# A fused attention, MLP and mixture-of-experts kernel: four weight conversions, a register load, transposes and low-part subtractions take other places in the expert phase

## The chip, the cores and the metric

The kernel runs on one core of a Trainium2 chip. Its engines are TensorE (PE in the profile: matmuls and transposes; its weight loads are PEld), VectorE (DVE), ScalarE (ACT), GpSimd (POOL) and SyncE (SP, which issues most transfers). Each engine works through its own instructions in program order; they meet by semaphores. The metric is device time in microseconds (us), the median of several executions.

## The reference

Three stages, each on 2304 tokens of 512 numbers:

```
# 1. attention, 4 x 8 heads, 576 positions of 64, a mask of blocks of 64
scores = np.where(mask, q @ kT * scale, -1e9); attn = softmax(scores); x = attn @ v
# 2. MLP, 512 -> 2048 -> 512
h = x @ w_in;  x = (max(h, 0) + alpha * min(h, 0)) @ w_out
# 3. mixture of 8 experts, 512 -> 1024 -> 512, one expert per token
logits = x @ w_gate;  expert_idx = argmax(logits);  gate_w = softmax(logits)[expert_idx]
for e in range(8):
    mask = expert_idx == e
    out[mask] = gate_w[mask, None] * (max(x[mask] @ w1[e], 0) @ w2[e])
```

## The kernel before

**Precision.** Most matmuls split each float32 operand into a high part (a rounded copy in the type fp32r) and a low part (the rest), and add three products: high by high, high by low, low by high (`pass3`). A weight block of 128 x 512 arrives by DMA in a tile `raw`; ScalarE casts it to the high part, then a subtraction on VectorE or GpSimd makes the low part. That pair is a conversion (`conv`). The tiles of the results are called `e`; an expert has 16 blocks, 0 to 7 for its first layer and 8 to 15 for its second.

**Up to the experts.** Attention and MLP are put in order by a planner (`Plan`), a list scheduler with a fixed cost per task. Its last tasks belong to the last of nine groups of 256 tokens. `first_expert` adds to the same plan the first expert's weights: 16 loads through four `raw` tiles in turn (`NR`), each followed by its conversion.

**The experts.** Behind the plan the program is written out in order by `Experts.run`. Experts come in the order of their token counts, the largest first (r = 0, 1, ...). An expert's tokens are worked in tiles of 256 (`tile256`, called by `body`), and what remains in a tile of 128 or 64. A tile gathers its tokens' rows from DRAM by an indirect DMA into `xg` (`fetch`; the list of rows `it` comes first, by a DMA on SP), turns them with TensorE transposes `Tx` (`xprep`), runs layer 1 (eight steps f, each twelve matmuls into `l`), then hidden values `hh` and `hl`, then layer 2 (two halves h of eight steps into `Y`, 0.70 us each at full clock), and scatters the scaled result to `out`. Between these steps `body` slips in two lists: `jobs`, the conversions of the next expert's weights, one per step; and `ahead`, of which one entry is taken behind every second step of layer 2: the eight places are f = 1, 3, 5, 7 of the first half, then of the second. Tiles that carry jobs have a + in their names.

**The first tile** (0, 0) is special. The last group's routing is done inside it, by hooks `at[n]`: transposes `rt` of the last group's outputs, copies of them back to `xg` (one half by ScalarE, one by VectorE), the gate's logits `lg` behind layer-1 step 1, the ranking matmul `rk` in step 3, two scatters of the token list `info`, then `fetch` of tile (0, 1), `order_all` (the order and the counts of the experts, on VectorE, into `odri`), `known` (SP reads the next expert's number, and the 16 loads of its weights are issued), and `counts` (every engine reads the eight counts into registers, and a branch hint for the branch `few0` that ends the tile).

**What sets the order.** Within an engine only the program order. SP's queue holds the lists `it` and the weight loads; POOL's the gathers and scatters, and its share of the low parts: `conv` sends blocks 2, 5, 8, 11, 14 of the later experts to GpSimd, the others to VectorE. Different paths for different counts are If blocks, each engine branching for itself. In this data the path is: expert 0 in five tiles of 256 (the third with jobs) and one of 128; expert 1 in two (the first with jobs) and one of 64; expert 2 in one with jobs and one of 64; expert 3 in a tile of 128 with jobs; expert 4 in one of 64.

Of the kernel before, what the change touches and what calls it, by code (L numbers as in the profile page):

```python
# [8 lines left out]
F32 = mybir.dt.float32  # L9
# [10 lines left out]
P = 128  # L20
# [11 lines left out]
NRECIP = 4  # L32
NR = 4
RATE = 300
LAG = 2
SC = 1.0 / float(D) ** 0.5
KC = 512 + P
# [254 lines left out]
class Attention:  # L292
# [24 lines left out]
    def plan(A, pl):  # L317
# [4 lines left out]
        for p, c in A.units():  # L322
            left.append(A.unit(pl, p, c, A.prio(p, c), A.soon(p, c), left))
            if (p < HP or A.soon(p, c)) and len(left) > LAG - 1:
                left.pop(0)()
# [21 lines left out]
    def early(A, pl):  # L347
# [3 lines left out]
        for p in range(2 * HP):  # L351
# [11 lines left out]

            got = pl.add(("SP", 450), load, [i], [x], pr + 10 * (p % HP), (P * 2 * EARLY * 4, RATE), [got] if b and p % 2 else ())
            pl.add(("ACT", 400), scale, [i], [x], pr + 5000 - 300 if b == 0 else pr + 600)
            if w not in pl.bufs:
# [5 lines left out]

                pl.add(("SP", 450), loadv, [], [w], pr + 10 * (p % HP) + 5, (131072 * n, RATE))

    def pair(A, pl, p):
# [14 lines left out]

        pl.add(("SP", 450), load, [], [("qk", p)], pr - 600 if p >= HP else 600 * p + 50, (P * QK * 4, RATE))
        pl.add(("SP", 450), loadv, [], [("v", p)], pr - 600 if p >= HP else 600 * p + 50, (327680, RATE))
        if plain:
# [21 lines left out]
    def unit(A, pl, p, c, pr, soon, left):  # L415
# [44 lines left out]
        fn, keys = scores1 if p < NPLAIN or soon else scores, Ss + [("step", 0)]  # L460
        if len(left) == LAG:
            left.pop(0)(ns, fn, ks, keys, pr)
# [466 lines left out]
class Experts:  # L929
# [53 lines left out]
    def conv(A, r, i):  # L983
        hi, lo = A.Ws[r % 2][i]
        raw = A.raw[r, i]
        A.nc.scalar.copy(hi, raw)  # L986
        (A.nc.gpsimd if i % (3 if r > 0 else 6) == 2 else A.nc.vector).tensor_sub(lo, raw, hi.bitcast(F32))  # L987

    def fetch(A, r, j, base, rows=NT + 1):
        it = A.itile(r, j)  # L990
# [164 lines left out]
    def run(A, base, last, order, order_all):  # L1155

        nc = A.nc

        def reg(row, r, top):
            return nc.sync.value_load(order.ri[0:1, row, r:r + 1], min_val=0, max_val=top)

        def xpreps(r, j):
            return [lambda: A.xprep(r, j, 0), lambda: A.xprep(r, j, 1)]

        def hint(label, cond):

            A.tc.mark_branch_hint_location(label, hint=cond, engines=ENGINES)

        def nexts(r, j, b, nb):
            fs = xpreps(r, j) if b is not None else []
            if nb is not None:
                fs += [lambda: A.fetch(r + 1, 0, nb)] + [lambda: None] * (4 - len(fs)) + xpreps(r + 1, 0)
            return fs

        def load_next(r):
            if r < E - 2:
                A.load_raws(r + 2, reg(0, r + 2, E - 1))

        def big(r, j, b, jobs=(), nb=None):
            more = A.TOP[r] > 2 * P * (j + 1)

            if A.TOP[r] > 2 * P * (j + 1) + P and (r, j) != (0, 1):
                hint(f"rest{r}_{j + 1}", ns[r] > 2 * P * (j + 1) + P)
            if more:
                A.fetch(r, j + 1, b)
            A.body(r, j, 2 * P, jobs, nexts(r, j + 1, b if more else None, nb))
            if jobs:
                load_next(r)  # L1190

        def bigs(r, j, b):
            if A.TOP[r] > 2 * P * j + P:
                with A.tc.If(ns[r] > 2 * P * j + P, label=f"rest{r}_{j}"):
                    big(r, j, b)
                    bigs(r, j + 1, b)

        def sized(n, left, go):

            def little():  # L1200
                with A.tc.If(left(0)):
                    go(64)

            if n > 64:
                with A.tc.If(left(64)) as c:
                    go(P)
                with c.Else():
                    little()
            else:
                little()  # L1210

        def remainder(r):

            n = (ns[r] + (P - 1)) & (2 * P - 1)

            def go(size):
                if r + 1 < E:
                    hint(f"less{r + 1}", ns[r + 1] <= P)
                A.body(r, 1, size, it=A.rem)

            sized(P if A.TOP[r] > 2 * P + 64 else 64, lambda k: n > P - 1 + k, go)

        def only(r, nb):

            jobs = [lambda: A.fetch(r + 1, 0, nb)] + [lambda i=i: A.conv(r + 1, i) for i in range(16)] if r < E - 1 else []
            if r < E - 2:
                jobs[-1] = lambda: (A.conv(r + 1, 15), load_next(r))

            def go(size):
                hint(f"more{r}", ns[r] > P)  # L1230
                A.body(r, 0, size, jobs, xpreps(r + 1, 0) if jobs else (), cond=ns[r + 1] > 0 if jobs else None)

            with A.tc.If(ns[r] <= 64) as c:  # L1233
                go(64)
            with c.Else():
                go(P)

        hold = {}

        def known():  # L1240
            hold["e1"], hold["nb"] = reg(0, 1, E - 1), reg(2, 1, (E - 1) * NT)
            A.load_raws(1, hold["e1"])
            A.wtiles(1)

        def counts():
            _, hold["n"] = nc.values_load_multi_w_load_instructions(order.ri[0:1, 1, :], min_val=0, max_val=NT)
            hint("few0", hold["n"][0] <= 5 * P)

        at = dict(last)
        for f in (lambda: A.fetch(0, 1, base), order_all, known, counts):  # L1250
            at[max(at) + 1] = f
        A.body(0, 0, 2 * P, [], [lambda: None] * 5 + xpreps(0, 1), at)
        nb = hold["nb"]
        ns = hold["n"]
        n0 = ns[0]

        def convs(r):
            return [lambda i=i: A.conv(r, i) for i in range(16)]

        with A.tc.If(n0 <= 5 * P, label="few0"):  # L1260
            with A.tc.If(n0 > 3 * P) as c:
                big(0, 1, base, convs(1), nb)
            with c.Else():
                for f in [lambda: A.fetch(1, 0, nb)] + convs(1) + xpreps(1, 0) + [lambda: load_next(0)]:
                    f()
            hint("many0", n0 > 5 * P)
        with A.tc.If(n0 > 5 * P, label="many0"):
            big(0, 1, base)
            big(0, 2, base, convs(1), nb)
            bigs(0, 3, base)  # L1270
        remainder(0)
        with ExitStack() as st:
            for r in range(1, E):
                base = nb
                st.enter_context(A.tc.If(ns[r] > 0))
                nb = reg(2, r + 1, (E - 1) * NT) if r < E - 1 else None
                jobs = convs(r + 1) if r < E - 1 else []
                with A.tc.If(ns[r] <= P, label=f"less{r}"):
                    only(r, nb)
                if r < E - 1:  # L1280
                    st.enter_context(A.tc.If(ns[r] + P * ns[r + 1] > P))
                with A.tc.If(ns[r] > P, label=f"more{r}"):
                    big(r, 0, base, jobs, nb)
                    bigs(r, 1, base)
                    remainder(r)


def moe_kernel(tc, qk, v, qke, ve, w_in, w_out, alpha, w_gate, w1, w2, out):
    nc = tc.nc
    with ExitStack() as ctx:  # L1290
# [15 lines left out]
        pl, banks, hold = Plan(), Slots(), {}  # L1306
# [7 lines left out]
        at = Attention(tc, qk, v, qke, ve, xT)  # L1314
# [38 lines left out]
        def first_expert(done):  # L1353
# [8 lines left out]
            def wload(i):  # L1362
                def f(on):
                    hold["ex"].wload(0, hold["e"], i, hold["ex"].raws[i % NR])
                pl.add(("SP", 450), f, [("e",)], [("raw0", i % NR)], 0, (262144, 180))

            def conv(i):
                pool = i % 6 == 2

                def hi(on):  # L1370
                    ex = hold["ex"]
                    ex.wtiles(0, i, i + 1)
                    nc.scalar.copy(ex.Ws[0][i][0], ex.raw[0, i])

                def lo(on):
                    ex = hold["ex"]
                    h, l = ex.Ws[0][i]
                    (nc.gpsimd if pool else nc.vector).tensor_sub(l, ex.raw[0, i], h.bitcast(F32))

                g, r = NG - 1, ("raw0", i % NR)  # L1380
                free = [("l1", g, 3 + 4 * (i // 8))] if i % 8 < 4 else [("l2", g, i // 8 * 4 + i % 4)]
                pl.add(("ACT", 600), hi, [r, *free], [("eh", i)] + ([("eh", i - 1)] if i else []), 1)
                pl.add(("POOL", 1600) if pool else ("DVE", 580), lo, [r, ("eh", i)], [("el", i)], 1)
# [6 lines left out]
            for i in range(NR):  # L1390
                wload(i)
            for i in range(16):
                conv(i)
                if i + NR < 16:
                    wload(i + NR)
            for i in range(GT):
# [19 lines left out]
        done = list(pl.tasks)  # L1416
        ml.plan(pl)
        first_expert(done)
        pl.emit()
        ex = hold["ex"]  # L1420
# [59 lines left out]
```

## Time and profile before

| | |
|---|---|
| time, median of 3 (lowest to highest) | 960.91 us (960.36 to 966.23) |
| the profiled execution | 963.68 us, span 961.9 us |
| PE busy | 898.5 us (93%) |
| DVE, ACT, POOL busy | 499.6 (52%), 410.0 (43%), 323.2 (34%) |
| mean granted TensorE clock | 0.971 of full speed |

The span runs from the first instruction to the last of the profiled execution; some 2 us of its time lie outside. The expert phase begins at about 652 us. A granted clock of 1.00 is TensorE's level of 2.4 GHz, 0.50 that of 1.2 GHz. Times of instructions overlap by a little, since a matmul's end is modelled.

### The profile page before, as it was taken

How to read it: one execution, taken by the hardware profiler on the slowest of the kernel's cores; microseconds unless marked ns; L12 is line 12 of the kernel's file. 1: busy time of each engine (PE TensorE's matmuls, PEld its weight loads, DVE VectorE, ACT ScalarE, POOL GpSimd, SP SyncE). 2: the span in 40 equal slices, each digit the busy share in tenths (PEclk: the TensorE clock that was granted, in tenths of full speed). 3: DMA queues.
4: the chain of work that ended last, by engine and by line, in shares of the span. 5: the costliest groups of instructions: out<-in, count | busy, mean ns of one | idle time of the engine just before them, and what ended most of it. 6: DMA issues, size and time to landing. Idle time of an engine off the chain costs nothing. (4 is left out here: it accounts for less than half of the span.)

```text
span 961.9 us, 17930 instructions
## 1 busy us (share of the span) xinstructions
PE 898.5 (93%) x6329; PEld 768.1 (80%) x6329; DVE 499.6 (52%) x1194; ACT 410.0 (43%) x1037; POOL 323.2 (34%) x333
## 2 busy tenths in 40 slices
PE   7998989999999999999999999998799998999874
PEld 6656658889888888888999999897698987888764
DVE  4999886656656556655444343455115211514360
ACT  6877765455455445545212121233125222524351
POOL 1455663323343433343223232331214212412340
PEclk9999989999999999999999999997899999999987
DMA  9981002212302122001001010151616211613451
GB/s 343 352 311 52 27 19 75 74 47 70 75 27 75 53 70 77 27 28 53 13 5 41 5 41 1 33 153 57 221 34 202 84 46 56 209 47 108 139 172 49
DMA packets 46268, 85.81 MB, mean 89 GB/s; under 512 B 12191, under 2 KB 18991, under 8 KB 46128
## 3 DMA queue, kind: packets, MB, share of 16 engines
q1 hardware_dynamic: 35264, 64.20, 20.9%
q0 software_dynamic: 4240, 11.56, 3.8%
q10 hardware_dynamic: 6624, 8.39, 2.4%
q8 instruction: 63, 1.03, 0.5%
q14 instruction: 77, 0.63, 0.2%
HBM read 70.85 MB, written 13.67 MB: 88 GB/s over the span
## 5 line engine op out<-in xcount | busy, mean ns | idle before, releaser
L692 PE MATMUL l<-xh,wi 128*128 128x256 f32 x1024 | 205.1, 286 | 0.0
L692 PEld LDWEIGHTS l<-xh,wi 128*128 128x128 f32 x1024 | 166.4, 190 | 4.2 <-issue 0.5
L720 PE MATMUL acc<-wo,gh 128*128 128x512 f32 x512 | 166.7, 407 | 0.0
L692 PE MATMUL l<-xl,wi 128*128 128x256 f32 x512 | 144.6, 282 | 0.1
L698 POOL TENSOR_TENSOR gl<-t,gh 128x256 fp32r<-128x256 f32 x103 | 78.4, 763 | 191.6 <-ACT gh L695 156.7
L670 DVE TENSOR_SCALAR t<-l,al 128x256 f32<-128x256 f32 x128 | 61.9, 484 | 139.3 <-PE l L692 136.1
L695 ACT CAST gh<-t 128x256 fp32r<-128x256 f32 x124 | 50.4, 406 | 184.3 <-DVE t L671 103.7
L528 POOL TENSOR_SCALAR P<-P,sm 128x256 f32<-128x256 f32 (+4 forms) x66 | 78.1, 1190 | 107.2 <-ACT gh L695 41.1
L720 PE MATMUL acc<-wo,gl 128*128 128x512 f32 x256 | 100.8, 394 | 2.7 <-POOL gl L698 2.7
L692 PEld LDWEIGHTS l<-xl,wi 128*128 128x128 f32 x512 | 97.5, 190 | 4.0 <-issue 0.5
L720 PEld LDWEIGHTS acc<-wo,gh 128*128 128x128 f32 x512 | 86.5, 190 | 11.2 <-issue 0.5
L477 DVE TENSOR_REDUCE nb<-S 128x1 f32<-128x256 f32 (+4 forms) x160 | 70.1, 477 | 41.0 <-PE S L454 25.9
L522 ACT COPY F<-PT 128x384 f32<-128x384 f32 (+2 forms) x124 | 57.3, 478 | 54.2 <-PE PT L517 52.8
L494 ACT ACTIVATE P<-S,nb 128x128 f32<-128x128 f32 (+3 forms) x128 | 66.9, 530 | 14.7 <-DVE nb L477 13.5
L517 PE MATMUL PT<-ident,P 128*128 128x128 f32 (+1 forms) x400 | 64.5, 281 | 7.8 <-DVE xo L571 5.4
L1030 PE MATMUL l<-cxh,e 128*128 128x256 f32 x320 | 62.9, 295 | 6.3 <-PEq L1260 4.3
L517 PEld LDWEIGHTS PT<-ident,P 128*128 128x128 f32 (+1 forms) x400 | 46.0, 141 | 21.1 <-DVE xo L571 5.0
L720 PEld LDWEIGHTS acc<-wo,gl 128*128 128x128 f32 x256 | 48.1, 188 | 14.9 <-POOL gl L698 4.0
L1030 PEld LDWEIGHTS l<-cxh,e 128*128 128x128 f32 x320 | 53.4, 202 | 7.1 <-issue 6.9
L671 DVE SCALAR_TENSOR_TENSOR t<-l,t 128x256 f32<-128x256 f32 x128 | 54.3, 425 | 4.4
L1030 PE MATMUL Y<-e,hh 128*128 128x512 f32 x176 | 56.3, 401 | 0.0
L987 DVE TENSOR_TENSOR e<-raw,e 128x512 fp32r<-128x512 f32 x44 | 40.2, 933 | 26.4 <-ACT e L986 26.3
(374 smaller groups left out, 1721.1 us busy)
## 6 DMA issues: line engine op xcount, KB each, us to landing
raw<-in_moe_w_dram SPq DMA_DIRECT2D x96, 256.0 KB, 3.7
qk<-in_qk_dram SPq DMA_DIRECT2D x16, 608.0 KB, 4.8
rawi<-in_moe_w_in_dram SPq DMA_DIRECT2D x16, 512.0 KB, 10.3
rawo<-in_moe_w_out_dram SPq DMA_DIRECT2D x16, 512.0 KB, 8.4
v<-in_v_dram SPq DMA_DIRECT2D x16, 320.0 KB, 3.2
x<-y ACTq DMA_DIRECT2D x16, 256.0 KB, 2.0
xr<-xT SPq DMA_DIRECT2D x7, 512.0 KB, 3.8
qe<-in_qke_dram SPq DMA_DIRECT2D x8, 256.0 KB, 4.4
```

The costliest lines, as they stand in the source:

```text
L477: nc.vector.tensor_reduce(pl["nb", p, c][:, 2 * k + j:2 * k + j + 1], pl[Ss[j]][:, a:b], axis=AX.X, op=ALU.max, negate=True)
L494: nc.scalar.activation(pl[x][:, a:b], pl[Ss[j]][:, a:b], AF.Exp, bias=nb, scale=1.0, accum_out=pl["sm", p, c][:, 2 * k + j:2 * k + j + 1])
L517: nc.tensor.transpose(pl[t][0:w, k], pl[x][:, P * k:P * k + w], A.K.ident)
L522: f(pl[F][:, 0:n], pl[t][:, 0:n])
L528: (nc.gpsimd if on == "POOL" else nc.vector).tensor_scalar(y, y, pl["sm", p, c][:, k:k + 1], None, op0=ALU.mult)
L670: nc.vector.tensor_scalar(pl[out], x, 0.0, A.K.al[:, f:f + 1], op0=ALU.min, op1=ALU.mult)
L671: nc.vector.scalar_tensor_tensor(pl[out], x, 0.0, pl[out], op0=ALU.max, op1=ALU.add)
L692: nc.tensor.matmul(pl[l][:, 0:G], lhsT=a[:, c], rhs=b, start=k == 0 and j == 0, stop=k == 3 and j == 2)
L695: (nc.scalar.copy if on == "ACT" else nc.vector.tensor_copy)(pl[gh], pl[t])
L698: (nc.gpsimd if on == "POOL" else nc.vector).tensor_sub(pl[gl], pl[t], pl[gh].bitcast(F32))
L720: nc.tensor.matmul(pl[acc], lhsT=x[:, c], rhs=w, start=f == 0 and j == 0, stop=f == 15 and j == 2)
L1030: A.nc.tensor.matmul(ps, lhsT=x[a], rhs=w[b], start=first and q == 0, stop=last and q == 2)
```

## The change

Four edits. The first expert's last four blocks (12 to 15, `FIRST`) are no longer converted in the plan but by hooks of the first tile (`late`), behind `known`. `counts` moves from a hook in layer 1 to the third place of `ahead`, and the loads of expert 1's weights move from `known` to the fourth, so behind `counts`. In later tiles the lists of `ahead` begin with an empty place (`nexts`), which puts every turn one place later, and the fetch for the next expert with it. All low parts go to VectorE.

```diff
         raw = A.raw[r, i]
         A.nc.scalar.copy(hi, raw)
-        (A.nc.gpsimd if i % (3 if r > 0 else 6) == 2 else A.nc.vector).tensor_sub(lo, raw, hi.bitcast(F32))
+        A.nc.vector.tensor_sub(lo, raw, hi.bitcast(F32))
...
         def nexts(r, j, b, nb):
-            fs = xpreps(r, j) if b is not None else []
+            fs = [lambda: None] + xpreps(r, j) if b is not None else []
             if nb is not None:
-                fs += [lambda: A.fetch(r + 1, 0, nb)] + [lambda: None] * (4 - len(fs)) + xpreps(r + 1, 0)
+                fs += [lambda: A.fetch(r + 1, 0, nb)]
+                fs += [lambda: None] * (6 - len(fs)) + xpreps(r + 1, 0)
...
             hold["e1"], hold["nb"] = reg(0, 1, E - 1), reg(2, 1, (E - 1) * NT)
-            A.load_raws(1, hold["e1"])
             A.wtiles(1)
...
+        def late(i):
+            A.wtiles(0, i, i + 1)
+            A.conv(0, i)
+
-        for f in (lambda: A.fetch(0, 1, base), order_all, known, counts):
+        for f in [lambda: A.fetch(0, 1, base), order_all, known] + [lambda i=i: late(i) for i in range(FIRST, 16)]:
             at[max(at) + 1] = f
-        A.body(0, 0, 2 * P, [], [lambda: None] * 5 + xpreps(0, 1), at)
+        ahead = [lambda: None] * 2 + [counts, lambda: A.load_raws(1, hold["e1"]), lambda: None] + xpreps(0, 1)
+        A.body(0, 0, 2 * P, [], ahead, at)
...
             for i in range(16):
-                conv(i)
+                if i < FIRST:
+                    conv(i)
                 if i + NR < 16:
```

The instructions of the plan keep their order on every engine; only the four conversions are taken out of it.

ScalarE in the first tile, before. `e_12` to `e_15` are the casts of the last four blocks, `xg<-rt` the copy that the logits need.

```order
L1373 CAST e_11_7959<-raw_6034 128x512
L1399 DMA x_58<-yo_6018 128x512
L1373 CAST e_12_7964<-raw_6031 128x512
L1373 CAST e_13_7967<-raw_6032 128x512
L1373 CAST e_14_7970<-raw_6033 128x512
L1373 CAST e_15_7973<-raw_6034 128x512
L861 COPY xg<-rt_0_8006 128x512
L814 ACTIVATE ex_8046<-L_8035 128x16
L1052 ACTIVATE hh_6023<-l_0_256_0_7993 128x512
```

The four casts stood ahead of the copy. The same stretch of ScalarE after the change:

```order
L1379 CAST e_11_7959<-raw_6034 128x512
L1406 DMA x_58<-yo_6018 128x512
L862 COPY xg<-rt_0_7994 128x512
L815 ACTIVATE ex_8034<-L_8023 128x16
L1053 ACTIVATE hh_6023<-l_0_256_0_7981 128x512
L1053 ACTIVATE hh_6025<-l_0_256_1_8046 128x512
L987 CAST e_12_8181<-raw_6031 128x512
L1053 ACTIVATE hh_6027<-l_0_256_2_8097 128x512
L987 CAST e_13_8193<-raw_6032 128x512
L987 CAST e_14_8202<-raw_6033 128x512
L987 CAST e_15_8211<-raw_6034 128x512
L1053 ACTIVATE hh_6029<-l_0_256_3_8186 128x512
```

The copy now follows the cast of block 11, and the four casts stand around the third and fourth `hh`; their subtractions stand in the same places on VectorE, behind `order_all`.

SP before, from the last of the 16 loads for expert 1 to the branch `few0` (`odri` is the tile of the counts):

```order
L976 DMA raw_7991<-in_moe_w_dram 128x512
L1246 TENSOR_LOAD odri
L1246 ISA x16
L1169 REGISTER_ALU
L1475 BRANCH_PREFETCH_HINT
L1260 COMPARE_AND_BRANCH
L1261 COMPARE_AND_BRANCH
```

SP read the counts behind its loads. After the change, from the reads of `known` to the first of the 16 loads:

```order
L1163 ISA x2
L1247 TENSOR_LOAD odri
L1247 ISA x16
L1170 REGISTER_ALU
L1482 BRANCH_PREFETCH_HINT
L977 ISA
L977 DMA raw_6031<-in_moe_w_dram 128x512
```

SP reads them first, and the loads start behind that. POOL reads them behind the gathers of tile (0, 1) in both.

VectorE in the tile of 128 of expert 3 (a + tile), up to the first `hl`, before. The branches stand around the jobs.

```order
L987 TENSOR_TENSOR e_0_7695<-raw_6031,e_0_7695 128x512
L987 TENSOR_TENSOR e_1_7727<-raw_6032,e_1_7727 128x512
L987 TENSOR_TENSOR e_3_7785<-raw_6034,e_3_7785 128x512
L1019 UNCONDITIONAL_BRANCH x2
L1019 COMPARE_AND_BRANCH
L987 TENSOR_TENSOR e_4_7811<-raw_7980,e_4_7811 128x512
L987 TENSOR_TENSOR e_6_7851<-raw_7982,e_6_7851 128x512
L1019 UNCONDITIONAL_BRANCH x2
L1082 TENSOR_TENSOR hl_6024<-Th_0_128+_0_14668,hh_6023 128x512
```

After the change:

```order
L988 TENSOR_TENSOR e_1_7727<-raw_6032,e_1_7727 128x512
L988 TENSOR_TENSOR e_2_7757<-raw_6033,e_2_7757 128x512
L988 TENSOR_TENSOR e_3_7785<-raw_6034,e_3_7785 128x512
L1020 UNCONDITIONAL_BRANCH x2
L1020 COMPARE_AND_BRANCH
L988 TENSOR_TENSOR e_4_7811<-raw_7968,e_4_7811 128x512
L988 TENSOR_TENSOR e_5_7832<-raw_7969,e_5_7832 128x512
L988 TENSOR_TENSOR e_6_7851<-raw_7970,e_6_7851 128x512
L1020 UNCONDITIONAL_BRANCH x2
L1083 TENSOR_TENSOR hl_6024<-Th_0_128+_0_14668,hh_6023 128x512
```

Seven subtractions now stand ahead of `hl` instead of five (block 0 is the row above the piece); blocks 2 and 5 have left GpSimd.

## Rows read from the trace of the kernel before

**Rows 1.** TensorE's timeline, 640 to 962 us: start, us, instruction [idle before, releaser]

```profile
658.56 3.59 PE L793 MATMUL lg<-wg,xg 128*128 128x8 f32 x16 [2.75 <-ACT xg L861]
...
673.14 0.36 PE L1030 MATMUL l<-cxh,e 128*128 128x256 f32 x1 [2.03 <-issue]
...
676.04 0.62 PE L1030 MATMUL Y<-e,hh 128*128 128x512 f32 x2
...
685.02 0.63 PE L1003 MATMUL Tx<-ident,xg 128*128 128x128 f32 x4 [0.42 <-DMA xg<-x,it]
...
688.09 0.63 PE L1003 MATMUL Tx<-ident,xg 128*128 128x128 f32 x4 [1.04 <-DMA xg<-x,it]
...
694.43 0.55 PE L1030 MATMUL l<-cxh,e 128*128 128x256 f32 x1 [4.31 <-PEq L1260]
...
733.96 0.63 PE L1003 MATMUL Tx<-ident,xg 128*128 128x128 f32 x4 [1.21 <-DMA xg<-x,it]
...
794.03 0.70 PE L1030 MATMUL H<-e,cxh 128*128 128x512 f32 x2 [1.17 <-ACTq L1194]
...
898.28 0.63 PE L1003 MATMUL Tx<-ident,xg 128*128 128x128 f32 x4 [0.88 <-DVE e L987]
...
925.32 0.80 PE L1030 MATMUL Y_128+_14687<-e,hl 128*128 128x512 f32 x1 [3.47 <-DVE hl L1082]
...
936.78 1.23 PE L1113 MATMUL H_64+_0_15724<-e,cxh 128*128 128x256 f32 x8 [2.10 <-DVEq L1282]
```

**Rows 2.** ScalarE's timeline, 655 to 659 us

```profile
657.40 0.62 ACT L1373 CAST e<-raw 128x512 fp32r<-128x512 f32 x1 [0.88 <-DMA raw<-in_moe_w_dram]
657.92 0.58 ACT L861 COPY xg<-rt 128x512 f32<-128x512 f32 x1
```

**Rows 3.** Windows: length, busy PE, PEld, DVE, ACT, POOL, granted clock, DMA share, GB/s

```profile
655.80:668.00 12.20, 9.45 (x45) 9.45 (x45) 4.31 (x19) 2.42 (x5) 1.48 (x2) 0.59 0.07 26
...
694.40:699.00 4.60, 4.57 (x22) 4.60 (x23) 0.00 (x0) 0.00 (x0) 0.00 (x0) 0.52 0.37 141
720.00:746.00 26.00, 24.80 (x163) 21.78 (x162) 13.62 (x20) 14.17 (x26) 11.82 (x11) 1.00 0.59 192
...
925.30:930.70 5.40, 5.38 (x19) 4.71 (x20) 2.20 (x4) 1.87 (x4) 0.00 (x0) 0.50 0.78 250
```

**Rows 4.** GpSimd's timeline, 668 to 682 us and 916 to 925 us

```profile
669.50 1.05 POOL L853 DMA_INDIRECT info<-ig,si  x1 [11.34 <-DVE ig L850]
673.22 0.98 POOL L853 DMA_INDIRECT info<-ig,si  x1 [2.67 <-DMA info<-ig,si]
679.94 0.98 POOL L996 DMA_INDIRECT xg<-x,it  x1 [5.74 <-DMA it<-info]
681.23 0.97 POOL L996 DMA_INDIRECT xg<-x,it  x1 [0.30 <-issue]
...
920.38 3.73 POOL L987 TENSOR_TENSOR e<-raw,e 128x512 fp32r<-128x512 f32 x3
```

**Rows 5.** SP's issues, 668 to 682 us

```profile
676.65 0.39 SPq L992 DMA_DIRECT2D it<-info  x1
...
679.38 2.67 SPq L976 DMA_DIRECT2D raw<-in_moe_w_dram  x5
```

**Rows 6.** VectorE's timeline, 668 to 682 us and 908 to 940 us

```profile
671.58 0.17 DVE L925 CAST odri<-odres 1x24 int32<-1x24 f32 x1
...
916.93 1.30 DVE L987 TENSOR_TENSOR e<-raw,e 128x512 fp32r<-128x512 f32 x2 [1.07 <-ACT e L986]
...
920.61 4.06 DVE L987 TENSOR_TENSOR e<-raw,e 128x512 fp32r<-128x512 f32 x1 [0.35 <-ACT e L986]
...
931.30 5.28 DVE L987 TENSOR_TENSOR e<-raw,e 128x512 fp32r<-128x512 f32 x5
```

**Rows 7.** DMA issues, 754 to 764 us: count, median us to landing

```profile
xg<-x,it POOLq DMA_INDIRECT x2, 3.3
```

**Rows 8.** DMA queues, 691 to 692 us: packets, MB, share of 16 engines

```profile
q8 instruction: 1, 0.02, 5.9%
```

## The prediction before the run

> **What bounds the kernel now.** TensorE is busy for 93% of the span, and up to 652 us the change leaves every instruction in its place, so I read only the expert phase, and there TensorE's idle time first: its timeline, for the rows that carry a bracket. [rows 1] holds those that the change can touch: 2.75 us ahead of the logits, 2.03 and 0.42 and 1.04 later in the first tile, 4.31 at the branch that ends it, 1.21 and 0.88 ahead of transposes, 3.47 and 2.10 around the tile of 128 of expert 3. The windows come second, for the granted clock: behind three of these waits TensorE ran at about its lower level, 0.59, 0.52 and 0.50 of full speed [rows 3], so such a wait costs more than its length. Third come the timelines of the engines named in the brackets, to see what stood in their queues.
>
> **The sum is made against the profiled execution**, 963.68 us with a span of 961.9; it lies 2.77 above the median of 960.91. I take the same number of microseconds off the median.
>
> **The first tile: logits.** ScalarE's copy of `xg` ran at 657.92, right behind the cast of the last block at 657.40, which itself waited for its transfer [rows 2]. TensorE had come to the logits at 655.81 (658.56 less 2.75). With the four casts out of the way the copy follows the transposes, which TensorE had finished well ahead of its step 1; the wait goes: 2.75 us. With it goes, I take it, the lower clock: between 655.80 and 668.00 TensorE was busy for 9.45 us, from the logits on all of it at half speed, which is 4.7 us at full. Some 4.05 of these 4.7 lie ahead of the end of `rk`, at 666.7 (8.1 us after 658.56, halved). So the end of `rk` moves by 2.75 + 4.05 = 6.8, to 659.9.
>
> **What is late next: the chain of the token list.** From `rk` two scatters of the list on POOL (669.50, 673.22) [rows 4], then the DMA of `it` on SP at 676.65 [rows 5], then the gathers at 679.94 and 681.23 follow each other, each waiting for the transfer before. None of these gaps holds work that the change takes out, so the chain keeps its length: gathers at 673.1 and 674.4. Their landing: before, the transposes could start 5.1 and 6.9 us after the issue (685.02, 688.09), with the weight loads in flight from 679.38; in a quiet stretch a gather lands in 3.3 us [rows 7]. The loads now wait for SP's read of the counts. SP's price for that shows in no row here; the nearest is TensorE's, which had `odri` at 671.75 [rows 6] and went on at 673.14, 1.39 later. Loads then start at 679.38 - 6.8 + 1.4 = 674.0, 0.9 behind the first gather instead of 0.6 ahead of it. For the first gather I take 3.9 us (between 3.3 and 5.1, nearer to quiet): 677.0. For the second, which meets the loads, 5.1 (between 3.3 and 6.9): 679.5.
>
> TensorE's own way from the end of `rk` to the first transpose was 684.60 - 666.7 = 17.9 us, with 2.03 of waiting at `counts` and 0.65 of low clock in it; without both it stands there at 675.1, and with a read of the counts of at most 1.39, which no longer waits for `odri`, at 676.5 at the latest. So the gathers bind: it waits 0.5 to 1.9 us for the first, then about 0.5 for the second (677.0 + 2.03 of work against 679.5), and ends at 679.5 + 2.03 = 681.5. Before it ended at 690.12 (694.43 less 4.31). **The first tile: 8.6 us less**; with both gathers as slow as before 6.8, with both in time and a free read 10.9 (675.1 + 4.06 = 679.2).
>
> **The four late conversions** cost nothing while their cover holds. VectorE ends `odri` 5.06 us after `rk`, at 665.0; then come four subtractions of 0.65 [rows 6] with two `hl` of the same size among them, 3.9 us in all: done at 668.9. Layer 2 starts at 676.04 - 666.7 - 2.03 - 0.65 = 6.7 after `rk`, at 666.6, and needs blocks 14 and 15 from its seventh step, at 666.6 + 6 x 0.70 = 670.8. The slack is 1.9 us; if `order_all` were slower, the excess would come on top, but under the gathers' wait it would cost nothing until 1 us more. The 16 loads that follow write tiles which these subtractions read last at 668.9, long before 674.0.
>
> **The branch `few0`.** I leave its 4.31 us, and the 2.3 us that the low clock behind it costs (4.57 busy at 0.52, halved). The instruction queue q8, which I take for TensorE's, moved no packet between 660 and 691 us, and one just after the branch [rows 8]: the target was fetched only once it was wanted, though the hint had been given some 17 us earlier. Giving it later in the tile does nothing that I can see for that.
>
> **Later turns.** At 733.96 TensorE waited 1.21 us for a gather; the transpose now stands one place, two layer-2 steps or 1.40 us, later: 1.2 gained. At 898.28 it waited 0.88; one place later too, and the gather ahead of it no longer stands behind a subtraction on POOL: 0.9 gained (0 if the wait was for VectorE, as the bracket says, and VectorE is later by what it has taken over). The last transposes of a + tile now end it; the tile that follows is of the same expert and uses other columns, so nothing waits for them.
>
> **Low parts on VectorE.** Twenty subtractions move, five in each of four + tiles, at 0.65 us each when GpSimd is quiet. In the tile of 128 of expert 3 VectorE's subtraction at 920.61 took 4.06 us while GpSimd ran three from 920.38 for 3.73 [rows 4, 6]; `hl` stood behind it, and TensorE waited 3.47. Now seven subtractions stand there, the last one ready when its cast is, at 920.6; at 0.65 each from 916.93 they end at 921.5, `hl` 0.7 later at 922.2. TensorE could go on at 922.3 instead of 925.32: 3.0 less, and the low clock behind (5.38 busy at 0.50) gives 2.7 more if it goes. Behind the two transposes of that tile VectorE has 7 subtractions instead of 5, but in 7 x 0.65 = 4.6 us instead of 5.28. The gather for the transposes was issued only at about 919, though, and may come at 924 to 926, where TensorE would now be at 924. **The two waits together: 4.5 us**, between 3.0 and 5.7. In the three tiles of 256 with jobs the cover is VectorE's idle time: it was busy 13.62 of 26.00 us there [rows 3], and five subtractions add 3.3.
>
> **Sum.** 8.6 + 1.2 + 0.9 + 4.5 = 15.2 us: 948.5 for the profiled execution, **945.7 for the median**.
>
> **The rivals.**
> *A, the hint works.* Given later, nearer to the branch, the hint may bring the target in time; the cheapest jump out of a tile is 1.17 us [rows 1]. Then 3.1 us go and the low clock behind (2.3): 945.7 - 5.4 = 940.3. Against it: no packet followed the old hint. The Trainium skill (Runtime: NRT & Kernel Launch, Instruction fetch mechanics) says that a taken branch whose target isn't in the small instruction window has to fetch it before going on; by that rule the 4.31 stays wherever the hint stands, and the trace's packet behind the branch agrees.
> *B, VectorE becomes the bound.* If in the + tiles the `hl` come behind the added subtractions and TensorE waits for each, all twenty are exposed, 20 x 0.69 = 13.8 us, and the 4.5 aren't gained: 960.91 - 8.6 - 2.1 + 13.8 = 964.0, slower than before. It decides once VectorE's work between two `hl` of such a tile exceeds TensorE's 2.85 us; by [rows 3] it would be 16.9 of 26, so it's far from there. The Trainium skill (Perfetto Trace Analysis, Optimizing Scalar/DVE Operations) advises giving work to GPSIMD when VectorE is saturated, which speaks against the move; the trace has VectorE at 52% in these tiles, so its condition isn't met, and the page itself doubts the offloading because of a shared read port.
> *C, the chain of the token list takes more back.* The waits for the gathers grow, or, three in 8 us, they bring the low clock with them: the first tile gains 4.3 (6.8 less 2.5), the tile of 128 only its 3.0: 960.91 - 4.3 - 2.1 - 3.0 = 951.5.
> *D, the low clock isn't due to the wait.* If the 16 narrow matmuls of the logits bring it even without a pause, the edit does only part of what it says: the end of `rk` moves by 2.75, the first tile by 8.6 - 4.05 = 4.5, and the time is 949.8.
>
> **How the numbers follow.** The forecast 0.56, A 0.14, B 0.05, C 0.14, D 0.11. The forecast's own bounds are 945.7 plus 1.8 + 0.9 + 1.5 = 949.9 and less 2.3 + 1.2 = 942.2. The range leaves out B, half of C and the far part of A: 939 to 951.5. About 1%, 9.6 us, is what a measurement of this kernel can tell from no change: faster than 951.3 are the forecast, A, D and part of C, 0.84 with something off for what I have not seen; within 1% 0.12; slower 0.04.
>
> **What would show it.** Right: in the first tile no wait ahead of the logits and clock 1.00 from there to the branch; waits of 0.5 to 2 us ahead of the two transposes; no wait of 2 us in layer 1; the branch still near 4.3; no VectorE subtraction above 0.8 us anywhere in the expert phase; TensorE's wait for `hl` in expert 3's tile under 1 us. Wrong: a clock of 0.5 behind the logits (D), waits for `hl` in the + tiles of 256 (B), a branch under 2 us (A), transposes that come after 683 (C).

## The result, and the profile after

| | before | after |
|---|---|---|
| median of 11 runs (lowest to highest) | 960.91 us (956.50 to 966.23) | 951.82 us (947.87 to 957.75) |
| ratio, 95% interval | | 0.9904 (0.9875 to 0.9932) |
| profiled execution, span | 963.68, 961.9 | 951.48, 949.7 |

The change makes the kernel 9.1 us faster by the medians, 12.2 by the two profiled executions. The forecast was 945.7 with a range up to 951.5; the time lies just above the range.

TensorE's timeline after, 650 to 962 us, the rows that answer to [rows 1], with the start of the logits and of tile (0, 2):

```profile
655.32 1.85 PE L794 MATMUL lg<-wg,xg 128*128 128x8 f32 x16
...
676.75 0.63 PE L1004 MATMUL Tx<-ident,xg 128*128 128x128 f32 x4 [2.15 <-DMA xg<-x,it]
...
681.64 0.36 PE L1031 MATMUL l<-cxh,e 128*128 128x256 f32 x1 [0.99 <-ACTq L1266]
...
700.06 1.09 PE L1004 MATMUL Tx<-ident,xg 128*128 128x128 f32 x4 [4.10 <-DMA xg<-x,it]
...
710.90 0.28 PE L1031 MATMUL l_256+_0_8960<-cxh,e 128*128 128x256 f32 x1
...
727.68 0.63 PE L1004 MATMUL Tx<-ident,xg 128*128 128x128 f32 x4 [0.37 <-DMA xg<-x,it]
...
864.54 0.58 PE L1031 MATMUL l_256+_0_13335<-cxh,e 128*128 128x256 f32 x1 [2.87 <-ACTq L1284]
...
915.43 0.80 PE L1031 MATMUL Y_128+_14687<-e,hl 128*128 128x512 f32 x1 [2.35 <-DVE hl L1083]
...
925.65 1.19 PE L1114 MATMUL H_64+_0_15724<-e,cxh 128*128 128x256 f32 x8 [2.10 <-ACTq L1020]
```

The wait of 2.75 ahead of the logits is gone, and the logits take 1.85 us instead of 3.59. The branch costs 0.99 instead of 4.31. New is 4.10 in tile (0, 1), where nothing waited before. Of the 3.47 at `hl`, 2.35 are left.

Windows after (length, busy PE, PEld, DVE, ACT, POOL, granted clock, DMA share, GB/s): behind the logits, behind the new wait, behind the wait for `hl`:

```profile
655.30:668.00 12.70, 12.70 (x103) 12.35 (x102) 9.62 (x40) 4.55 (x9) 2.31 (x2) 1.00 0.09 34
700.00:707.00 7.00, 6.94 (x28) 5.73 (x29) 1.71 (x3) 1.86 (x3) 0.48 (x1) 0.76 0.06 25
...
915.40:920.80 5.40, 5.37 (x23) 4.58 (x24) 2.96 (x6) 2.41 (x5) 0.00 (x0) 0.72 0.98 326
```

The low clock behind the logits [rows 3] is gone with the wait; part of it stands behind the new wait.

SP's issues after, 660 to 700 us, and GpSimd's gathers in the same stretch:

```profile
670.96 0.38 SPq L995 DMA_DIRECT2D rem<-info  x1
676.04 11.93 SPq L977 DMA_DIRECT2D raw<-in_moe_w_dram  x16
693.94 0.39 SPq L993 DMA_DIRECT2D it<-info  x1
```

```profile
673.37 0.98 POOL L997 DMA_INDIRECT xg<-x,it  x1 [5.81 <-DMA it<-info]
...
696.54 0.99 POOL L997 DMA_INDIRECT xg<-x,it  x1 [13.07 <-DMA it<-info]
```

The loads now start 5.1 us behind `rem`, where they started 2.2 behind it (679.38 [rows 5] less 677.23): SP's read of the eight counts, with the hint behind it, costs 2.9 us. The list of tile (0, 2) stands behind 11.9 us of loads and SP's own branch. It moved from 698.36 to 693.94, 4.4 us, while TensorE's start of tile (0, 1) moved 12.8, and so the gathers come late.

By stages, from the starts of TensorE's rows in both traces (the first transposes of tile (0, 0) at 648.29 and 647.96):

| stage | before | after | gained | forecast |
|---|---|---|---|---|
| first tile and branch | 46.14 | 33.68 | 12.46 | 8.6 |
| tile (0, 1) | 25.50 | 29.26 | -3.76 | 0 |
| tile (0, 2) to expert 0's remainder | 74.10 | 73.14 | 0.96 | 1.2 |
| remainder and expert 1's tiles of 256 | 67.33 | 67.96 | -0.63 | 0 |
| expert 1's tile of 64 and the jump behind it | 11.52 | 12.54 | -1.02 | 0 |
| expert 2's tile of 256 | 30.79 | 30.63 | 0.16 | 0.9 |
| expert 2's tile of 64 | 11.01 | 10.75 | 0.26 | 0 |
| expert 3's tile of 128 | 22.10 | 19.73 | 2.37 | 4.5 |
| to the end of the span | 25.12 | 24.05 | 1.07 | 0 |

With 0.33 ahead of the first stage that is 12.2 us. In expert 3 VectorE's row is this (before, its first subtraction started 1.07 us behind its last `yo`, at 916.93 [rows 6]); ScalarE's casts for it began at 907.45:

```profile
906.63 0.47 DVE L1136 SCALAR_TENSOR_TENSOR yo<-Y,rem,yo 64x256 f32<-64x256 f32 x1 [0.96 <-ACT yo L1135]
910.46 4.31 DVE L988 TENSOR_TENSOR e<-raw,e 128x512 fp32r<-128x512 f32 x7 [3.36 <-ACT yo L1075]
914.69 0.69 DVE L1083 TENSOR_TENSOR hl<-Th_128+_0_14668,hh 128x512 fp32r<-128x512 f32 x1
```

Seven subtractions take 4.31 us, and none takes 4 us any more; but the first starts 3.36 us behind the last `yo` of VectorE. The releaser that the row names, a `yo` of ScalarE, is nothing that a subtraction needs: in the kernel before, ScalarE began that `yo` at 918.44, and the subtractions had started at 916.93.

### The profile page after: what moved, and what is told of

The parts are those of the page before. It is cut to its first block, busy times and chain, and to the rows that moved or that the text cites. A ratio compares the mean times of both kernels' runs of the same rounds, so it can differ in the third digit from the quotient of the medians.

```text
span 949.7 us, 17897 instructions
## 1 busy us (share of the span) xinstructions
PE 892.8 (94%) x6329; PEld 763.4 (80%) x6329; DVE 499.5 (53%) x1215; ACT 409.7 (43%) x1037; POOL 294.1 (31%) x312
## 5 line engine op out<-in xcount | busy, mean ns | idle before, releaser
L1031 PE MATMUL l<-cxh,e 128*128 128x256 f32 x320 | 58.3, 282 | 1.0 <-ACTq L1266 1.0
L988 DVE TENSOR_TENSOR e<-raw,e 128x512 fp32r<-128x512 f32 x68 | 43.9, 686 | 21.4 <-ACT e L987 17.8
L562 PE MATMUL o<-F,v 128*64 128x128 f32 (+2 forms) x832 | 53.4, 264 | 0.0
```

What stands on the lines that cost most here:

```text
L562: nc.tensor.matmul(y, lhsT=v[0:w, 2 * kc + h], rhs=f, start=kc == 0, stop=kc == c, skip_group_check=True)
L1031: A.nc.tensor.matmul(ps, lhsT=x[a], rhs=w[b], start=first and q == 0, stop=last and q == 2)
```

## The experiments

One kernel's time scatters by about 5 us to either side, part of it ahead of the expert phase (its first transposes start between 645.87 and 651.04 in the 14 traces), so the medians (of five or six runs, twelve for the two kernels built on the one before) settle only large differences. For the rest I compare stages of the traces.

**1. The loads later** (on the changed kernel):

```diff
-        ahead = [lambda: None] * 2 + [counts, lambda: A.load_raws(1, hold["e1"]), lambda: None] + xpreps(0, 1)
+        ahead = [lambda: None] * 2 + [counts, lambda: None, lambda: None] + xpreps(0, 1)
...
                 A.fetch(r, j + 1, b)
+            then()
             A.body(r, j, 2 * P, jobs, nexts(r, j + 1, b if more else None, nb))
...
-            big(0, 1, base)
+            big(0, 1, base, then=lambda: A.load_raws(1, hold["e1"]))
```

> The changed kernel, but the 16 loads of expert 1's weights are issued in tile (0, 1), behind the list and the gathers of tile (0, 2), instead of in the first tile. Theory (SP's queue): the 4.10 us for which TensorE waits at the transposes of tile (0, 1) come from SP, where `it` of tile (0, 2) stands behind 11.9 us of loads and 6 us of branch. Then SP issues `it` before 683 us instead of 693.94, the gathers start before 687 instead of 696.54, the wait falls below 0.5 us, the clock from 700 to 707 us is 1.00 instead of 0.76, tile (0, 2) starts some 5 us earlier (near 706 instead of 710.90), and the time is about 947 where the changed kernel has 951.8. Rival (the gathers are held up by something else on GpSimd, or the loads now collide with them): the wait stays within 1 us of 4.1 and the time within 1.5 us of 951.8.

Measured: 946.35 us (945.89 to 951.44). SP issues `it` of tile (0, 2) at 682.47, the gathers start at 686.24, no wait is left in tile (0, 1), and its window has clock 1.00:

```profile
700.00:707.00 7.00, 7.00 (x33) 5.70 (x32) 1.23 (x3) 1.28 (x2) 1.03 (x1) 1.00 0.18 70
```

From the first transposes to the start of tile (0, 2) it takes 59.60 us instead of 62.94. So SP's queue was the cause of the 4.10. The branch waits 2.04 here, not 0.99.

**2. No hint** (on 1):

```diff
-            hint("few0", hold["n"][0] <= 5 * P)
```

> The kernel with the loads in tile (0, 1), and the hint for the branch few0 taken out on every engine; the counts are read where they were. Theory (the hint, given late in layer 2, brings the branch's target in time): without it TensorE waits about 4.3 us at the branch instead of 1.0, with a granted clock near 0.5 behind it, and the time is 4 to 6 us longer than that of the kernel with the loads in tile (0, 1). Rival (the code happens to lie better, the hint plays no part): the wait at the branch stays within 0.5 us of 1.0 and the time is the same within 1 us.

Measured: 946.69 us (945.34 to 951.51); the branch waits 2.13, against 2.04 in 1. The theory falls: the hint plays no part.

**3. The counts early** (on 1):

```diff
-        for f in [lambda: A.fetch(0, 1, base), order_all, known] + [lambda i=i: late(i) for i in range(FIRST, 16)]:
+        for f in [lambda: A.fetch(0, 1, base), order_all, known, counts] + [lambda i=i: late(i) for i in range(FIRST, 16)]:
...
-        ahead = [lambda: None] * 2 + [counts, lambda: None, lambda: None] + xpreps(0, 1)
+        ahead = [lambda: None] * 2 + [lambda: None] * 3 + xpreps(0, 1)
```

> The kernel with the loads in tile (0, 1), but the counts are read, and the hint given, in layer 1 behind `known`, as before the change. Theory (the place of the hint decides: too early it is lost): the wait at the branch is back at 4 us or more with a clock near 0.5 behind it, no instruction packet of queue q8 moves between the hint and the branch, TensorE waits again 1 to 2 us for the counts in layer 1, and the time is 5 to 7 us longer than with the counts in layer 2. Rival (a hint works wherever it stands, what mattered was something else in the code): the wait at the branch stays near 1.0 and only the wait for the counts is added, at most 2 us.

Measured: 944.0 us (943.35 to 947.38). TensorE waits 2.30 for the counts, then for no gather, and 0.82 at the branch. The place of the hint doesn't matter either, and moving the counts bought nothing: its 2.3 us return as the 2.12 for the gathers in 1.

**4. Low parts back on GpSimd** (on the changed kernel):

```diff
-        A.nc.vector.tensor_sub(lo, raw, hi.bitcast(F32))
+        (A.nc.gpsimd if r > 0 and i % 3 == 2 else A.nc.vector).tensor_sub(lo, raw, hi.bitcast(F32))
```

> The changed kernel with the low parts of every third block of the later experts back on GpSimd. In the tile of 128 of expert 3 the changed kernel has VectorE's first subtraction 3.0 us behind the first cast, and TensorE waits 2.35 us for `hl`. Theory (VectorE starts late because it fetches its code there, whatever its work is): the late start of about 3 us stays, a subtraction of about 4 us returns on VectorE while GpSimd runs its three, TensorE's wait for `hl` is 3.4 to 5 us, and the time is 1 to 4 us longer than the changed kernel's. Rival (the late start comes with the added subtractions): VectorE's first subtraction starts within 1 us of the first cast's end, the wait for `hl` is about 3.5 as before the change, and the time 1 to 1.5 us longer.

Measured: 950.9 us (946.28 to 953.37), no difference that the medians can show. VectorE starts 1.07 us behind its last `yo`, the 4.07-us subtraction is back, `hl` costs 3.50, and expert 3's tile takes 22.10 us, as before the change. So the rival holds for the late start: it comes with VectorE's low parts. The 1 to 1.5 us that it added to the time do not show. The branch costs 4.21 again, though nothing ahead of it differs from the changed kernel: its code, or the loads in flight.

**5. The kernel before with the loads later** (the edit of 1).

> The kernel before, with one edit: the 16 loads of expert 1's weights are issued in tile (0, 1), behind the list and the gathers of tile (0, 2). Theory (the branch's code is fetched by the same DMA engines as the weights, and waits behind the 16 loads): the packet of queue q8 then moves about 1.0 us behind the start of the last transposes instead of 3.3, and TensorE, which goes on some 3.1 us behind that packet, waits 2.0 to 2.3 us at the branch instead of 4.31; the gathers of tile (0, 1) land sooner, so that the waits of 0.42 and 1.04 grow by at most 0.5 in all or vanish; the time is 3 to 5 us below that of the kernel before. Rival (the wait comes from how the code lies, which the low parts on VectorE changed): 4.2 to 4.4 us at the branch and at most 2 us gained.

Measured: 955.66 us (952.69 to 959.05), ratio 0.9941 (0.9919 to 0.9962). The branch waits 0.82, the gathers not at all, and the way to tile (0, 2) falls from 71.64 to 64.80 us. Here is what these kernels do at the branch. "Work ends" is the end of what TensorE does ahead of it; "packet" is the time, to some 0.2 us, at which queue q8, taken for TensorE's instruction queue, moved its packet:

| kernel | loads start | work ends | packet | TensorE goes on | wait |
|---|---|---|---|---|---|
| before | 679.38 | 690.12 | 691.3 | 694.43 | 4.31 |
| 4, GpSimd | 677.11 | 684.27 | 685.5 | 688.48 | 4.21 |
| after | 676.04 | 680.65 | 678.1 | 681.64 | 0.99 |
| 1, loads later | 684.45 | 680.52 | 679.5 | 682.56 | 2.04 |
| 2, no hint | 688.19 | 683.65 | 682.5 | 685.78 | 2.13 |
| 3, counts early | 688.80 | 685.46 | 682.7 | 686.28 | 0.82 |
| 5, before, loads later | 693.28 | 689.84 | 687.2 | 690.66 | 0.82 |

Wherever the wait is over 1 us, TensorE goes on 3.0 to 3.3 us behind the packet; this holds too for the waits of 1.72, 2.04, 4.55 and 1.24 us in 8, 10, 11 and 12. With no loads in flight, and in the changed kernel, where they had begun 2.1 us before it, the packet moves 0.9 to 1.4 us behind the start of transposes (the second ones in 1 and 2, the first ones in the others). Where the loads fill the queues, it moves 3.2 and 4.1 us behind the second ones. The same stretch of 0.4 us or less around the packet, in the kernel before and in 5:

```profile
q1 hardware_dynamic: 87, 0.16, 101.3%
q8 instruction: 1, 0.02, 14.7%
```

```profile
q8 instruction: 1, 0.02, 33.2%
```

Weights (q1) filled the engines in the one, the code had them alone in the other. In 11, where the loads stand as in the kernel before, the wait is 4.55. That the packet of the changed kernel came in time because its loads had just begun is argued from this table, not shown.

**6. No late conversions** (on 3):

```diff
-FIRST = 12
+FIRST = 16
```

> The kernel with the loads in tile (0, 1) and the counts in layer 1, with the last four blocks of the first expert converted in the plan again, as before the change. Theory (the wait ahead of the logits and the low clock behind it go together, as the prediction priced them): a wait of 2.5 to 3 us ahead of the logits, a granted clock near 0.6 behind it, the end of `rk` 6.8 us later, and, with the gathers binding behind it, a time 6 to 7 us above the 944.0 of that kernel. Rival (the low clock there does not depend on the wait): the end of `rk` 2.8 us later, and the time 2.5 to 3.5 us above.

Measured: 951.8 us (949.01 to 955.30), 7.8 above 3. TensorE's row for the logits:

```profile
660.29 3.58 PE L794 MATMUL lg<-wg,xg 128*128 128x8 f32 x16 [2.65 <-ACT xg L862]
```

From the first transposes to the end of `rk` it takes 17.6 us instead of 11.8, to the start of tile (0, 2) 64.46 instead of 58.81; the granted clock from 657.60 to 668.00 is 0.67. The wait and the low clock go together, worth 5.7 us by the stage.

**7. GpSimd's low parts, loads out of the way** (the edit of 4 on 3).

> The kernel with the loads in tile (0, 1) and the counts in layer 1, with the low parts of every third block of the later experts back on GpSimd. Theory (the move of the low parts gains 1.1 us at `hl` in expert 3 and gives it back at jumps, where the engines fetch more code): the time is the same as with VectorE's low parts within 1.5 us, 942.5 to 945.5; VectorE starts within 1 us of the first cast's end in expert 3; the wait at the jump to expert 2's tile of 256 falls from 2.9 to about 1.9. Rival (the prediction's price): 3.0 to 5.7 us above, 947 to 950. It also shows whether the branch few0 gets its code late with GpSimd's low parts even without the loads in the way: about 0.8 to 2.2 us of waiting if the loads were the cause, 4.2 if the place of the code was.

Measured: 949.59 us (945.74 to 952.49), 5.6 above 3, as the rival had it; by the stage it is less, 21.97 us for expert 3's tile instead of 19.90. The branch waits 0.82, so the place of the code was not its cause. The jump to expert 2's tile costs 2.69, not the 1.9 that I expected.

**8. The tile of 128 first** (on 3):

```diff
-            with A.tc.If(ns[r] <= 64) as c:
-                go(64)
-            with c.Else():
-                go(P)
+            with A.tc.If(ns[r] > 64) as c:
+                go(P)
+            with c.Else():
+                go(64)
```

> The kernel with the loads in tile (0, 1) and the counts in layer 1, with the two branches for an expert of at most 128 tokens in the other order: the tile of 128 first, the tile of 64 behind it. Nothing else changes. Theory (VectorE's start 3.5 us late in expert 3 is the fetch of its code behind a jump across the tile of 64): the jump falls away, VectorE's first subtraction starts within 1.2 us of its last `yo`, TensorE's wait for `hl` falls from 2.5 to under 0.5 us, and the time is 2 to 5 us below 944.0. Rival (it waits for something else, ScalarE's `yo` as the page says): the idle time stays at 3.3 us or more and the wait for `hl` at 2 us or more.

Measured: 941.67 us (939.51 to 950.05), 2.3 below 3 by the medians; but the ratios to the kernel before, given at the end of this section, are nearly the same for both, so what it gains is read from the stage. VectorE's and TensorE's timelines in expert 3:

```profile
894.89 0.48 DVE L1136 SCALAR_TENSOR_TENSOR yo<-Y,rem,yo 64x256 f32<-64x256 f32 x1 [0.96 <-ACT yo L1135]
896.08 4.53 DVE L988 TENSOR_TENSOR e<-raw,e 128x512 fp32r<-128x512 f32 x7 [0.71 <-ACT e L987]
```

```profile
901.26 0.50 PE L1031 MATMUL Y_128+_14507<-e,hl 128*128 128x512 f32 x1 [0.27 <-DVE hl L1083]
905.79 0.63 PE L1004 MATMUL Tx<-ident,xg 128*128 128x128 f32 x4 [2.46 <-issue]
```

VectorE now waits only for its cast, and `hl` costs 0.27. In the changed kernel queue q14 moved two packets from 907 to 908 us, just behind VectorE's last `yo`; here it moved none from 893 to 898:

```profile
q14 instruction: 2, 0.02, 4.9%
```

So the late start was the jump across the tile of 64, whose code had grown with the low parts. That q14 carries VectorE's code, and that its fetch is what VectorE waited for, is inferred; in the kernel before q14 moved one packet there, from 916.0 to 916.5, and VectorE started in time. The tile takes 18.55 us instead of 19.90, with 2.46 of new waiting at the second transposes in it.

**9. The turns back** (on 8):

```diff
-            fs = [lambda: None] + xpreps(r, j) if b is not None else []
+            fs = xpreps(r, j) if b is not None else []
...
-                fs += [lambda: None] * (6 - len(fs)) + xpreps(r + 1, 0)
+                fs += [lambda: None] * (4 - len(fs)) + xpreps(r + 1, 0)
```

> The kernel with the loads in tile (0, 1), the counts in layer 1 and the branches in the other order, with the later turns undone: the lists of `ahead` of the later tiles begin with the transposes again, as before the change. Theory (the prediction's price): the waits ahead of the transposes of tile (0, 2) and of expert 2's tile grow by 1.2 and 0.9 us, and the time by some 2 us from 941.7. Rival (the turns were covered, or the gather lands so late that the wait is only shifted to the second transposes): at most 0.5 us more waiting in these two tiles together, and the time the same within 1 us.

Measured: 942.56 us (941.52 to 945.52), no difference. In tile (0, 2) the transposes wait 1.53 and 0.39 instead of 0.17 and 0.87, 0.88 more in all; in expert 2 neither kernel waits. The rival is nearer. Expert 3's tile, which the edit doesn't touch, takes 17.24 us here instead of 18.55, with 1.38 of waiting at its second transposes instead of 2.46: so much can differ between two profiles of the same code there.

**10. GpSimd's low parts** (the edit of 4 on 8).

> The kernel with the loads in tile (0, 1), the counts in layer 1 and the branches in the other order, with the low parts of every third block of the later experts back on GpSimd. With VectorE no longer late, this prices the move of the low parts as the prediction meant it. Theory (the prediction's term holds where VectorE starts in time): a subtraction of about 4 us on VectorE in expert 3's tile, TensorE's wait for `hl` 3.0 to 3.6 us instead of 0.27, a granted clock near 0.5 behind it, and the time 3.0 to 5.7 us above 941.7. Rival (what is gained at `hl` is lost again at the transposes behind it, which wait for their gather): the wait for `hl` as above, but the wait of 2.46 at the transposes gone, and the time at most 1.5 us above.

Measured: 948.81 us (944.16 to 950.95), 7.1 above 8. `hl` costs 3.48, the wait at the transposes is gone, and the tile takes 21.17 us instead of 18.55: 2.6 by the stage, between the two theories. By the medians it is more than either says, but by the ratios to the kernel before (0.9853 against 0.9824) it is 2.8 us, so the whole time doesn't settle which holds. VectorE starts 0.71 us behind its last `yo`, as in 8: without the jump it is in time with either sharing of the low parts.

**11. The kernel before with VectorE's low parts alone**:

```diff
-        (A.nc.gpsimd if i % (3 if r > 0 else 6) == 2 else A.nc.vector).tensor_sub(lo, raw, hi.bitcast(F32))
+        A.nc.vector.tensor_sub(lo, raw, hi.bitcast(F32))
```

> The kernel before, with one edit: all low parts on VectorE. Theory (VectorE is late in expert 3 whenever all sixteen low parts of the skipped tile of 64 stand in its code): VectorE's first subtraction 3.3 us or more behind its last `yo`, TensorE's wait for `hl` 2.3 to 2.6 us instead of 3.47, and the time 0.5 to 2.5 us below the kernel before. Rival (the prediction's price): the wait for `hl` under 0.6 us and 3.0 to 5.7 us below.

Measured: 957.74 us (953.39 to 961.50), ratio 0.9948 (0.9923 to 0.9972), 4.2 us. VectorE is 3.43 us late, `hl` costs 2.42, the tile takes 19.93 instead of 22.10. The mechanism is the theory's, with 2.2 us of it in that tile; the time is more than that, part of it at the jump to expert 2's tile of 64, 1.81 us instead of 3.36 in these profiles.

**12. Loads in another order** (on 8; `load_next` passes the list on to `load_raws`):

```diff
-                jobs[-1] = lambda: (A.conv(r + 1, 15), load_next(r))
+                jobs[-1] = lambda: (A.conv(r + 1, 15), load_next(r, [*range(8, 16), *range(8)]))
```

> The kernel with the loads in tile (0, 1), the counts in layer 1 and the branches in the other order; in the tile of an expert of at most 128 tokens the 16 loads for the expert after the next are issued in the order of blocks 8 to 15, 0 to 7, so that SP's first load waits for the conversion of block 8. Theory (the 2.46 us ahead of expert 3's second transposes come from gathers that share the DMA engines with loads issued at the same time): the loads start some 5 us later, the gathers land within 4 us, the wait of 2.46 falls under 0.7, and the time is 1.5 to 3 us below 941.7. Rival (the gather or the transposes are held up by something else, `issue` as the page says): the wait stays above 2 us and the time the same within 1 us.

Measured: 946.04 us (942.06 to 950.53), 4.4 above 8 by the medians, where the theory had it 1.5 to 3 below; the intervals of the ratios, 0.9797 to 0.9852 here, overlap. SP's first load stands 8.5 us behind the tile's start (901.44, 909.92) instead of 2.7 (894.19, 896.90), the gathers are in time, the 2.46 are gone, as the theory says, and the wait at the jump behind the tile grows from 2.12 to 5.32:

```profile
920.58 2.05 PE L1114 MATMUL H_64+_0_15905<-e,cxh 128*128 128x256 f32 x8 [5.32 <-DVEq L1290]
```

TensorE's packet came at 917.1, 3.5 us earlier, amid the loads, and the tile takes 19.14 us instead of 18.55. In 8 the gathers came late beside the weight loads, here the code did.

Among the kernels that beat both the one before and the changed one are 3, 8 and 9: their ratios to the kernel before of 0.9816 (0.9784 to 0.9848), 0.9824 (0.9783 to 0.9864) and 0.9799 (0.9774 to 0.9825).

## Why the prediction was off

Right were the end of `rk` (6.75 us earlier by the traces, 18.56 to 11.81 from the first transposes; forecast 6.8), the low clock that goes with the wait (so not rival D), and the gathers as what is late next: TensorE waited 2.15 for the first and ended the tile's work at 680.65, against a forecast of 681.5. In the + tiles of 256 no `hl` made TensorE wait (not rival B), and no subtraction took 4 us. The time is nearly rival C's 951.5, but by chance: C had the first tile gain 4.3 us, and it gained 12.46.

Four steps failed.

- **"I leave its 4.31 us."** The branch fell to 0.99, rival A's result by another mechanism. I read the packet [rows 8] as fetched only when wanted, whatever stands elsewhere. In these runs it is fetched ahead, 0.3 to 1.4 us behind the start of transposes, unless weight loads fill the DMA engines (5 and 7). The Trainium skill (Runtime: NRT & Kernel Launch, Instruction fetch mechanics) has a branch out of the window wait for its code; the trace agrees, 3.1 us from packet to work. What I hung on it, that the 4.31 must stay, does not follow.
- **"None of these gaps holds work that the change takes out"** was right for the gathers of tile (0, 1), and there I stopped. The next list, of tile (0, 2), stood behind the loads on SP, and these started at 676.04, not 674.0: SP's read costs 2.9 us where I took 1.4. It ended last as soon as TensorE came 12.8 us earlier, and took 3.76 back. This and the first failure nearly cancel: to tile (0, 2) the gain was 8.7, and that this is the forecast's 8.6 is luck.
- **"The two waits together: 4.5 us"** was 2.37. I let the seven subtractions start where the old five did, at the cast; the code of the tile that is jumped over had grown as well, and VectorE came 2.3 us later (3.36 less 1.07). Where it comes in time (8 and 9), the tile gains 3.55 and 4.86 against before, inside the 3.0 to 5.7.
- **Later turns**, 1.2 and 0.9, came to 0.96 and 0.16: waits of 0.15 and 0.37 remain in tile (0, 2), and in expert 2's tile the clock was lower in this profile (0.89 for 0.94 over the stage), which took back most of the 0.88 that vanished. This stage took 26.4 to 30.8 us in the 14 traces, at clocks from 0.89 to 1.00, so one pair of profiles cannot price 0.9 us in it. Experiment 9 prices the turns at 0.9 us of waiting, and the time did not change.

Together with the 1.0 us that the jump to expert 2's tile grew by, and small differences in the stages where nothing was forecast, these make 11.9 us instead of 15.2. The rest of the miss is the reference: I took a sum read from a run 2.77 us above its median off that median, while the profiled run after lies 0.34 below its own. The bounds held nothing for that.

Two things stay open. The jump to expert 2's tile of 256 costs 1.86 or 1.87 us in the kernel before and in 4, 5 and 11, 2.7 to 2.9 in the other ten, and no one edit separates these. And what the low parts on VectorE gain in the whole time is not settled: expert 3's tile gains 2.1 to 2.6 us in each of the four pairs (4, 7, 10, 11), but the medians give nothing, 5.6, 7.1 and 4.2.

## What to carry to other kernels

When an edit makes one engine 12 us earlier, follow each queue that feeds its next tile, not only the one that feeds this: here a block of weight loads on the queue of the small lists gave back 3.8 us, and moving it behind the next list gained 5.5 us by the medians in either kernel. Count code as traffic: here a jump's target came over the same DMA engines as the weights, and VectorE, which jumps across the tile of 64, paid for the code added to it. Make a range wide enough for the run that the sum was read from.

## What the runs showed of the hardware

A branch hint changed nothing that can be measured: with it late, early or gone the wait was 2.04, 0.82 and 2.13 us, and TensorE went on 3.1, 3.6 and 3.3 us behind its packet. Reading eight counts into registers, with the hint behind it, cost SP 2.9 us (5.1 less 2.2); TensorE's 2.3 in layer 1 (3) show nowhere when the read stands in layer 2, where it has work queued. In expert 3's tile VectorE's first subtraction stood 3.4 to 3.5 us behind its last `yo` in each of the six kernels that have all low parts on VectorE and the tile of 64 first, 1.05 to 1.07 in each of the four with GpSimd's part and that order, where it waited for its cast, and 0.71 in the four with the tile of 128 first, whatever the low parts.
